# Attention with two gated MLPs on one core: two score tiles in one pair of banks, the 1e-9 added by GpSimd, the reciprocals transposed in the accumulator, and a new table of the order

## The chip, the cores and the metric

The kernel runs on one core of one Trainium2 chip. The metric is the device time of one execution in microseconds, as the median of several runs. A compute core has five engines with their own instruction streams: TensorE (PE; its weight loads are listed apart as PEld), VectorE (DVE), ScalarE (ACT), GpSimd (POOL) and SyncE (SP), which here does nothing but issue DMAs. Each engine works through its own stream in order and waits for the others by semaphores; what stands behind a waiting instruction on the same engine waits too.

## What is computed

Three stages follow each other. The first is attention with forget gates (4 batches, 8 heads, 576 positions, 64 per head), then a two-matrix MLP with softplus, then a gated MLP with a sigmoid:

```
cum    = cumsum(log(clip(f, 1e-4, 1)))
scores = q @ k.T / 8 + cum[i] - cum[j], causal
attn   = exp(scores - rowmax); attn = attn / (sum(attn) + 1e-9)
x = (attn @ v), heads side by side          # 2304 x 512
x = softplus(x @ w_in) @ w_out              # 512 -> 2048 -> 512
y = (sigmoid(x @ w_gate) * (x @ w_val)) @ w_out2
```

The weights come in as 64-bit floats and everything is computed in float32 precision: each operand is kept as a high and a low part, and a product is the sum of three matmuls.

## The kernel before

**Attention.** The 32 heads are worked through as 16 pairs, p = 0 to 15. For each pair SP loads q, k and v (`load_q`, `load_k`, `load_v`), two decay rows per head from DRAM (`decay_rows`), and POOL splits them into high and low parts (`qh`, `ql`, `kh`, `kl`, `v_high`, `v_low`). `scores` makes nine score tiles of a pair: tile i of head 0 and tile 8 - i of head 1 together for i = 0 to 3 (two PSUM banks with the tag "s", one per head, each head on 64 of the 128 rows of PE), and tile 4 for both heads in two other banks. `minimum` (DVE) adds the mask and takes the row minimum of the negated scores, `exp` (ACT) makes the exponentials and their row sums. `transposes` (PE) turns blocks of the exponentials in groups 0 to 6, `evac_h` (ACT) and `evac_l` (DVE) copy the two parts out, and `pv` (PE) multiplies by v into the accumulators `acc0` and `acc1`, which hold the transposed output of one head each.

**The reciprocals.** The output is divided by the row sums only at the end. `rinv` on DVE adds the 1e-9 (line 304, from a tile `eps` of constants) and takes the reciprocal (line 305) of 128 x 9 sums; `rinv_t` transposes them on PE into a bank of its own with the tag "t" (line 310), which it shares with the groups of `transposes`; `rinv_b` copies them to SBUF on ACT; `rinv_c` stores them to DRAM (line 319) and `rinv_d` reads them back spread over 64 partitions per head (line 325), which needs the store to have landed. `out_a` (ACT) and `out_b` (DVE) empty the accumulators, `out_c` (POOL, line 366) multiplies by the reciprocals, and `out_d` stores to the DRAM tensor xT in three DMAs (lines 373 to 375).

**Weights and tokens beside it.** While attention runs, `Weights.op` prepares the first weight blocks of the first MLP in seven steps: a load (SP, line 498), SCALE (ACT), SHIFT, LOW and SIGN (DVE, lines 520, 522, 524), HI (ACT) and LO (POOL, line 514). Ten blocks may be scaled at most before the first MLP's own loop takes over. `Tokens.step` loads the first 512 finished rows of xT (line 560) and splits them, in four chunks.

**The order.** All DMAs of attention go through SP's one queue, and all engine streams follow from the order in which the Python code emits the steps. `run` sorts the steps by a number: 9 per pair plus an entry of the table WHEN, or of START for pair 0 and END for pair 15; weights, tokens and the first two units of the first MLP have their own lists (STEPS, LATE_STEPS, X_STEPS, PRODUCTS, UNITS). Only the order of these numbers counts.

**The start.** `begin` loads the gates, makes the decay sums on DVE and ACT, and prepares pair 0's q and k. `busy` issues matmuls on a tile of zeros (line 47), 28 in all, that do no part of the computation and keep PE at work in the waits of pair 0. POOL meanwhile builds masks, the identity and other constants.

Of the kernel before, what the change touches and what calls it, by code (L numbers as in the profile page):

```python
# [9 lines left out]
F32 = mybir.dt.float32  # L10
# [3 lines left out]
ALU = mybir.AluOpType  # L14
# [7 lines left out]
class Attention:  # L22


    S = 576
# [17 lines left out]

    def busy(self, n):
# [7 lines left out]
    def begin(self):  # L52
# [12 lines left out]
        self.busy(14)  # L65
# [18 lines left out]
        nc.vector.tensor_scalar(hi, cum, -8.0, m[0:66], op0=ALU.mult, op1=ALU.mult)  # L84
        nc.vector.scalar_tensor_tensor(lo, cum, -8.0, f, op0=ALU.mult, op1=ALU.subtract)
        nc.sync.dma_start(self.nb[:, 0], c[32:64, 0:S])
        nc.sync.dma_start(self.nb[:, 1], lo[32:64].bitcast(F32))
        self.kl(P0, 0)
        self.sub(None, self.buf(P0, 0, "Xl", 640), P0["qr"], P0["Xh"], "V")
        self.constants2()  # L90

    def constants(self):
# [21 lines left out]
        self.eps = c.tile([128, 9], F32, name="eps")  # L114
        nc.gpsimd.memset(self.eps, 1e-9)
# [91 lines left out]
    def scores(self, R, p, i):  # L207
# [18 lines left out]
        w = self.W9[i]  # L226
        N = max(w, 256)
        ps = [self.ps.tile([128, 512], F32, tag="s", bufs=2, name=f"s{p}_{i}_{h}") for h in range(2)]
        q = slice(128 * i, 128 * i + 128)
        if p == 0:  # L230
            self.busy({2: 1, 3: 2}.get(i, 0))
        for j, (L, r) in enumerate(((Xh[:, q], Yh), (Xl[:, q], Yh), (Xh[:, q], Yl), (self.one[:, 0:128], nb))):
            if p == 0 and i == 1 and j == 1:
                self.busy(4)
            for h in range(2):
                o = slice(64 * h, 64 * h + 64)
                nc.tensor.matmul(ps[h][:, 0:N], L[o], r[o, 0:N], start=j == 0, stop=j == n - 1)  # L237
        for h in range(2):
            R["src", (i, 8 - i)[h]] = R["P"], ps[h][:, 0:w], self.mask[:, 512 - w:512]
# [22 lines left out]
    def transposes(self, R, p, g):  # L262
        nc = self.nc
        ps = R["T", g] = self.ps.tile([128, 512], F32, tag="t", bufs=2, name=f"t{p}_{g}")
        for n, (t, j) in enumerate(self.GROUPS[g][0]):
            if p == 0 and n == 1 and g == 3:
                self.busy(5)
            elif p == 0 and n == 0 and g == 5:
                self.busy(2)
# [98 lines left out]
    def out_d(self, R, p):  # L368
# [18 lines left out]
        ("minimum", 6): 5.8865, ("exp", 0): 6.2356, ("minimum", 2): 6.379, ("exp", 1): 6.6423, ("exp", 4): 6.7033,
        ("exp", 2): 7.105, ("transposes", 0): 7.5695, ("load_v",): 7.7728, ("exp", 6): 7.8053,
        ("transposes", 1): 7.9929, ("exp", 8): 8.7191, ("evac_h", 0): 9.5166, ("evac_h", 1): 9.5706,
        ("rinv",): 10.083, ("v_high",): 10.1126, ("evac_l", 0): 10.4436, ("v_low",): 10.514,  # L390
        ("evac_l", 1): 11.2219, ("transposes", 2): 12.2269, ("evac_h", 2): 12.276, ("transposes", 3): 12.3519,
        ("evac_h", 3): 12.4099, ("evac_l", 2): 13.0431, ("rinv_t",): 13.1193, ("rinv_b",): 13.2113,
        ("evac_l", 3): 13.7368, ("transposes", 5): 13.8096, ("transposes", 4): 13.9726, ("evac_h", 5): 14.8574,
        ("pv", 0, 0): 14.9016, ("evac_h", 4): 14.9515, ("evac_l", 5): 15.137, ("pv", 0, 2): 15.291,
        ("evac_l", 4): 15.6663, ("transposes", 6): 15.699, ("evac_h", 6): 16.5991, ("evac_l", 6): 16.839,
        ("pv", 0, 4): 17.6509, ("pv", 0, 3): 18.0197, ("pv", 0, 1): 18.5838, ("pv", 1, 0): 18.8295,
# [784 lines left out]
```

## Time and profile before

| what | value |
|---|---|
| median of 3 runs | 1022.93 us (1022.85 to 1024.15) |
| the profiled execution's own time | 1021.91 us |
| its span, first to last instruction | 1020.0 us |
| PE / PEld / DVE / ACT / POOL busy | 1006.7 / 883.1 / 610.7 / 510.4 / 147.7 us |
| DMA | 196.07 MB, 192 GB/s over the span |

Busy time of an engine is the union of its instructions; PE's matmuls overlap and their ends are modelled, so a PE that is shown as busy may still be held up inside. A row of an engine's instructions in order of time gives the start in us, the duration in us, the engine and line, the operation, out<-in with the program's names, the shape, the count, and in brackets the idle time before it and who ended it. Stretches of time are given from the start of the span. SP's rows are DMA issues.

### The profile page before, as it was taken

The numbers are of one execution on the slowest core, as the hardware profiler recorded it, in microseconds if no ns is written. First come the engines' busy times: TensorE is split into PE (matmuls) and PEld (weight loads), VectorE is DVE, ScalarE is ACT, GpSimd is POOL, SyncE is SP. The second block draws the span as 40 slices with busy tenths as digits, with TensorE's granted clock in tenths as the row PEclk, the third lists the DMA queues.
The fourth block names the chain that finished last, engine by engine and source line by source line (L and its number), as shares of the span: only waits on it lengthen the run. The fifth ranks groups of instructions, "written<-read, shape, count | busy, mean of one in ns | idle before, by whom it ended". The sixth has DMA issues, their size and how long they took to land.

```text
span 1020.0 us, 15929 instructions
## 1 busy us (share of the span) xinstructions
PE 1006.7 (99%) x5612; PEld 883.1 (87%) x5612; DVE 610.7 (60%) x1227; ACT 510.4 (50%) x1085; POOL 147.7 (14%) x154
## 2 busy tenths in 40 slices
PE   8999999999999999999999999999999999999998
PEld 6888878878788889988888889999999999999997
DVE  6999999879855766545626744544344344343333
ACT  5888888866644445435434443333333333333332
POOL 8677776610000000000000000000000000000000
PEclk9999999999999999999999999999999999999999
DMA  4455555545636566635526767766676666576641
GB/s 138 139 148 150 153 149 146 146 139 186 210 120 212 203 219 229 233 125 216 211 89 199 265 226 266 271 217 210 218 264 237 229 217 222 200 249 219 215 144 62
DMA packets 114698, 196.07 MB, mean 192 GB/s; under 512 B 14702, under 2 KB 38398, under 8 KB 114620
## 3 DMA queue, kind: packets, MB, share of 16 engines
q1 hardware_dynamic: 112684, 189.98, 55.8%
q10 hardware_dynamic: 1936, 5.09, 1.6%
q8 instruction: 44, 0.72, 0.3%
q14 instruction: 34, 0.28, 0.1%
HBM read 149.19 MB, written 45.83 MB: 191 GB/s over the span
## 4 chain that ended last, share of the span: by engine, by line
PE 86%; DVE 5%; ACT 2%; issue 2%; DMA 2%; POOL 2%; SPq 1%; ACTq 0%; POOLq 0%; DVEq 0%
PE z L577 9%; PE z L579 9%; PE z L578 9%; PE h L578 5%; PE h L577 5%; PE h L579 5%; PE x L348 4%; PE s L237 4%; PE t L272 4%; PE oY L578 2%; PE oY L577 2%; PE oY L579 2%; PE oX L578 2%; PE oX L579 2%; PE oX L577 2%
## 5 line engine op out<-in xcount | busy, mean ns | idle before, releaser
L577 PE MATMUL z<-three,three 128*128 128x384 f32 x456 | 152.9, 335 | 0.1
L579 PE MATMUL z<-three,three 128*128 128x384 f32 x456 | 152.9, 335 | 0.0
L578 PE MATMUL z<-three,three 128*128 128x384 f32 x456 | 152.7, 335 | 0.0
L626 DVE TENSOR_TENSOR gl<-L,gh 128x512 fp32r<-128x512 f32 (+1 forms) x80 | 51.0, 638 | 107.9 <-ACT gh L625 104.1
L614 ACT ACTIVATE L<-h 128x512 f32<-128x512 f32 (+1 forms) x80 | 44.3, 554 | 141.5 <-PE h L579 141.4
L577 PEld LDWEIGHTS z<-three,three 128*128 128x128 f32 x456 | 85.6, 188 | 2.0 <-DVE raw L887 0.5
L249 ACT ACTIVATE P<-P,m 128x128 f32<-128x128 f32 (+3 forms) x144 | 83.1, 581 | 7.3 <-DVE m L244 7.3
L578 PEld LDWEIGHTS z<-three,three 128*128 128x128 f32 x456 | 85.6, 188 | 1.3
L579 PEld LDWEIGHTS z<-three,three 128*128 128x128 f32 x456 | 85.6, 188 | 0.0
L244 DVE CUSTOM_DVE_ANT_0 P<-s,mask 128x256 f32<-128x256 f32 (+3 forms) x144 | 70.6, 517 | 9.9 <-PE s L237 5.9
L577 PE MATMUL h<-xh,wi_h 128*128 128x512 f32 (+1 forms) x200 | 73.7, 368 | 0.0
L579 PE MATMUL h<-xh,wi_h 128*128 128x512 f32 (+1 forms) x200 | 73.6, 368 | 0.0
L578 PE MATMUL h<-xl,wi_h 128*128 128x512 f32 (+1 forms) x200 | 73.6, 368 | 0.0
L298 DVE TENSOR_TENSOR PTl<-t,PTh 128x512 fp32r<-128x512 f32 (+2 forms) x112 | 66.8, 619 | 4.3 <-ACT PTh L294 4.2
L874 ACT COPY bl<-z 128x384 f32<-128x384 f32 x36 | 17.3, 480 | 102.4 <-PE z L579 102.4
L886 DVE TENSOR_TENSOR raw<-z,bh 128x384 f32<-128x384 f32 x36 | 20.1, 558 | 76.7 <-PE z L579 76.7
L879 DVE TENSOR_TENSOR raw<-z,p 128x384 f32<-128x384 f32 x18 | 10.0, 558 | 93.2 <-PE z L579 79.3
L294 ACT CAST PTh<-t 128x512 fp32r<-128x512 f32 (+2 forms) x112 | 55.9, 537 | 16.7 <-PE t L272 16.2
L272 PE MATMUL t<-ident,P 128*128 128x128 f32 x400 | 58.6, 280 | 3.5 <-DVE PTl L298 3.2
L908 ACT CAST gh<-raw 128x384 fp32r<-128x384 f32 x72 | 33.5, 513 | 49.0 <-DVE raw L891 47.6
L272 PEld LDWEIGHTS t<-ident,P 128*128 128x128 f32 x400 | 43.6, 140 | 16.2 <-issue 4.4
L348 PE MATMUL x<-PTh,V 128*128 128x256 f32 (+2 forms) x224 | 56.4, 312 | 0.5 <-POOL V L181 0.5
(296 smaller groups left out, 2577.1 us busy)
## 6 DMA issues: line engine op xcount, KB each, us to landing
three<-sd_g SPq DMA_DIRECT2D x126, 256.0 KB
three<-sd_v SPq DMA_DIRECT2D x126, 256.0 KB
two<-sd_w SPq DMA_DIRECT2D x36, 256.0 KB
raw_wi<-in_moe_w_in_dram SPq DMA_DIRECT2D x16, 512.0 KB
raw_wo<-in_moe_w_out_dram SPq DMA_DIRECT2D x16, 512.0 KB
fraw<-in_moe_w_gate_dram SPq DMA_DIRECT2D x12, 512.0 KB
fraw<-in_moe_w_out_dram SPq DMA_DIRECT2D x12, 512.0 KB
sd_g<-sh SPq DMA_DIRECT2D x24, 256.0 KB
```

What stands on the lines that cost most here:

```text
L237: nc.tensor.matmul(ps[h][:, 0:N], L[o], r[o, 0:N], start=j == 0, stop=j == n - 1)
L244: self.nc.vector.tensor_tensor_reduce(P, src, mask, -0.125, 3e38, op0=ALU.add, op1=ALU.min, accum_out=R["m"][:, t:t + 1])
L249: self.nc.scalar.activation(P, P, AF.Exp, bias=R["m"][:, t:t + 1], scale=-1.0, accum_out=R["sum"][:, t:t + 1])
L272: nc.tensor.transpose(ps[:, 128 * n:128 * n + 128], R["P"][:, o:o + 128], self.ident)
L294: self.nc.scalar.copy(d, s)
L298: self.nc.vector.tensor_sub(l, s, h)
L348: nc.tensor.matmul(R["acc%d" % h][:, o:o + n], v, t[:, col:col + n], start=j == 0 and w == 0, stop=j == 1 and w == 1)
L577: nc.tensor.matmul(ps, ah, bh, start=start and i == 0, stop=False, **how)
L578: nc.tensor.matmul(ps, ah, bl, start=False, stop=False, **how)
L579: nc.tensor.matmul(ps, al, bh, start=False, stop=stop and i == n - 1, **how)
L614: nc.scalar.activation(g, ph, AF.Softplus)
L626: nc.vector.tensor_sub(gl, s, gh)
```

## The change

The scores of tile 0 are written behind those of tile 1 in the same two banks (columns 256 to 511), in one call: `scores` with i = 1 now does both, and `scores` 0 is gone from the tables. The 1e-9 is added by POOL (`rinv_a`, a new step with a place of its own); DVE keeps the reciprocal. `rinv_t` writes to the first 128 columns of the pair's `acc0`, which `pv` uses from column 256 on, and not to a bank of tag "t". In `begin`, the low part of pair 0's k goes from POOL to DVE and stands with that of q ahead of the low half of the decay sums; the loads of q and k of pair 1 are issued there too. The tables are new throughout; so are the places of the idle matmuls (30). Ten weight blocks are allowed from the start, and the numbers of STEPS bring three steps of six blocks to pairs 2 to 8.

```diff
-    def rinv(self, R, p):
-        nc = self.nc
-        r = self.sm.tile([128, 9], F32, tag="r", name=f"r{p}")
-        nc.vector.tensor_add(r, R["sum"], self.eps)
-        nc.vector.reciprocal(r, r)
-        R["r"] = r
+    def rinv_a(self, R, p):
+        R["r"] = self.sm.tile([128, 9], F32, tag="r", name=f"r{p}")
+        self.nc.gpsimd.tensor_scalar(R["r"], R["sum"], 1e-9, 1.0, op0=ALU.add, op1=ALU.mult)
+
+    def rinv(self, R, p):
+        self.nc.vector.reciprocal(R["r"], R["r"])
 
     def rinv_t(self, R, p):
-        ps = self.ps.tile([128, 512], F32, tag="t", bufs=2, name=f"rt{p}")
-        self.nc.tensor.transpose(ps[0:9, 0:128], R["r"], self.ident)
-        R["rt"] = ps
+        R["acc0"] = self.wide.tile([128, 1024], F32, tag="Y", name=f"x{p}_0")
+        self.nc.tensor.transpose(R["acc0"][0:9, 0:128], R["r"], self.ident)
...
+        for x, a in ((1, 0), (0, 256)) if i == 1 else ((i, 0),):
+            w = self.W9[x]
+            N = max(w, 256)
+            q = slice(128 * x, 128 * x + 128)
+            for j, (L, r) in enumerate(((Xh[:, q], Yh), (Xl[:, q], Yh), (Xh[:, q], Yl), (self.one[:, 0:128], nb))):
...
+                    nc.tensor.matmul(ps[h][:, a:a + N], L[o], r[o, 0:N], start=j == 0, stop=j == n - 1)
...
         nc.vector.tensor_scalar(hi, cum, -8.0, m[0:66], op0=ALU.mult, op1=ALU.mult)
+        nc.sync.dma_start(self.nb[:, 0], c[32:64, 0:S])
+        P1 = self.R[1] = {}
+        self.load_q(P1, 1)
+        self.load_k(P1, 1)
+        self.sub(None, self.buf(P0, 0, "Yl", S), P0["kr"], P0["Yh"], "V")
+        self.sub(None, self.buf(P0, 0, "Xl", 640), P0["qr"], P0["Xh"], "V")
         nc.vector.scalar_tensor_tensor(lo, cum, -8.0, f, op0=ALU.mult, op1=ALU.subtract)
-        nc.sync.dma_start(self.nb[:, 0], c[32:64, 0:S])
         nc.sync.dma_start(self.nb[:, 1], lo[32:64].bitcast(F32))
-        self.kl(P0, 0)
-        self.sub(None, self.buf(P0, 0, "Xl", 640), P0["qr"], P0["Xh"], "V")
...
-    W.limit = EARLY
+    W.limit = EARLY + MORE
...
-        ("kl",): -9.0904, ("decay_rows",): -8.1126, ("scores", 4): -2.7503, ("scores", 3): -2.135,
...
-        ("rinv_c",): 19.6722, ("rinv_d",): 19.9764, ("pv", 1, 2): 20.0352, ("out_a", 0): 21.1841,
...
+        ("kl",): -0.1247, ("decay_rows",): 2.4063, ("scores", 4): 5.4379, ("scores", 3): 7.3316,
...
+        ("rinv_c",): 32.2841, ("out_b", 1): 32.2934, ("rinv_d",): 34.4816, ("out_c",): 39.1994, ("out_d",): 45.4318}
```

Below, the engines' order at three places in the middle of attention. In names like rd_1495 the number counts buffers in the built program.

SP, one period of the queue before, from one pair's store of the reciprocals (rd) to the next pair's loads (xT is the output of an earlier pair, qr, kr and vr are q, k and v, nb the decay rows):

```order
L319 DMA rd_1687<-rt_sb_1561 9x128
L325 DMA rb_1689<-rd_1687 64x576 x2
L373 DMA xT<-xs_1519 64x576
L374 DMA xT<-xs_1519 64x64
L375 DMA xT<-xs_1519 64x4x128
L148 DMA qr_124<-in_q_dram 64x576
L149 DMA qr_124<-in_q_dram 64x512
L150 DMA qr_124<-in_q_dram 64x64
L161 DMA vr_184<-in_v_dram 128x4x128
L162 DMA vr_184<-in_v_dram 64x128
L185 DMA nb_129<-nb_d 2x576 x2
L156 DMA kr_1869<-in_k_dram 64x576 x2
```

and the same period now:

```order
L316 DMA rd_1587<-rt_sb_1421 9x128
L159 DMA kr_1606<-in_k_dram 64x576 x2
L322 DMA rb_1632<-rd_1587 64x576 x2
L370 DMA xT<-xs_1345 64x576
L371 DMA xT<-xs_1345 64x64
L372 DMA xT<-xs_1345 64x4x128
L188 DMA nb_133<-nb_d 2x576 x2
L164 DMA vr_191<-in_v_dram 128x4x128
L165 DMA vr_191<-in_v_dram 64x128
L151 DMA qr_126<-in_q_dram 64x576
L152 DMA qr_126<-in_q_dram 64x512
L153 DMA qr_126<-in_q_dram 64x64
```

The load of k moved to between the store of the reciprocals and the read that needs it, and the decay rows moved to behind the stores of xT.

DVE around the reciprocals before (PTl is what `evac_l` writes, P what `minimum` writes):

```order
L244 ISA P_1023,m_1024<-s_3_1_1047,mask 128x512
L244 ISA m_1024 128x1
L304 TENSOR_TENSOR r_1103<-sum_830,eps 128x9
L305 RECIPROCAL r_1103<-r_1103 128x9
L298 TENSOR_TENSOR PTl<-t_0_1058,PTh 128x512
```

DVE now, and after it POOL around the step that makes r_939:

```order
L360 TENSOR_TENSOR xs_954<-x_0_801,bs_955 64x576
L296 TENSOR_TENSOR PTl<-t_2_934,PTh 128x512
L304 RECIPROCAL r_939<-r_939 128x9
L296 TENSOR_TENSOR PTl<-t_3_945,PTh 128x2x256
L360 TENSOR_TENSOR xs_954<-x_1_903,bs_955 64x576
```

```order
L184 TENSOR_TENSOR Yl_879<-kr_833,Yh_877 128x576
L184 TENSOR_TENSOR V_842<-vr_189,V_842 128x10x64
L301 TENSOR_SCALAR r_939<-sum_626 128x9
L363 TENSOR_TENSOR xs_761<-xs_761,rb_859 128x576
```

The addition left DVE, and the reciprocal now stands behind a step of POOL that itself follows the low parts of k and v.

PE at score tile 0 before, after a block of `pv` on all 128 rows and ahead of the transpose of the reciprocals:

```order
L348 MATMUL x_1_1092<-PTl,V_911 128x256
L237 MATMUL s_0_0_1163<-Yh_878,Xh_849 128x256
L237 MATMUL s_0_1_1164<-Yh_878,Xh_849 128x256
L237 MATMUL s_0_0_1163<-Yh_878,Xl_882 128x256
L237 MATMUL s_0_1_1164<-Yh_878,Xl_882 128x256
L237 MATMUL s_0_0_1163<-Yl_885,Xh_849 128x256
L237 MATMUL s_0_1_1164<-Yl_885,Xh_849 128x256
L237 MATMUL s_0_0_1163<-nb_130,one 128x256
L237 MATMUL s_0_1_1164<-nb_130,one 128x256
L310 MATMUL rt_1174<-ident,r_1103 9x128
L272 MATMUL t_5_1182<-ident,P_828 128x128 x4
```

and now, from the end of tile 1 to the end of the first two terms of tile 0:

```order
L239 MATMUL s_1_0_1110<-nb_133,one 128x256
L239 MATMUL s_1_1_1111<-nb_133,one 128x256
L239 MATMUL s_1_0_1110<-Yh_877,Xh_871 128x256
L239 MATMUL s_1_1_1111<-Yh_877,Xh_871 128x256
L239 MATMUL s_1_0_1110<-Yh_877,Xl_873 128x256
L239 MATMUL s_1_1_1111<-Yh_877,Xl_873 128x256
```

Tile 0's eight matmuls moved to directly behind tile 1's, so PE goes from 128 rows to 64 and back three times per pair, and not four.

## Rows read from the trace of the kernel before

**Rows 1.** Busy time by stretch: length, PE, PEld, DVE, ACT, POOL (instructions), PE clock, DMA share, GB/s.
```profile
28.69:122.24 93.55, 93.35 (x750) 78.29 (x749) 89.53 (x240) 83.72 (x233) 66.48 (x59) 1.00 0.52 143
122.24:184.68 62.44, 59.39 (x475) 49.39 (x473) 59.40 (x158) 53.17 (x146) 45.72 (x39) 1.00 0.52 148
184.68:296.92 112.24, 110.14 (x559) 91.31 (x558) 92.18 (x173) 73.06 (x140) 14.70 (x12) 1.00 0.50 167
296.92:1020.00 723.08, 719.24 (x3696) 646.54 (x3694) 350.24 (x611) 285.32 (x532) 0.00 (x0) 1.00 0.60 208
```
**Rows 2.** PE in order of time: first matmul of score tile 4, pairs 2, 3, 15.
```profile
28.69 0.40 PE L222 MATMUL s<-Yh,Xh 128*128 128x288 f32 x1
...
40.22 0.29 PE L222 MATMUL s<-Yh,Xh 128*128 128x288 f32 x1
...
184.68 0.29 PE L222 MATMUL s<-Yh,Xh 128*128 128x288 f32 x1
```
**Rows 3.** SP in order of time, 100.57 to 111.90: one period of the queue.
```profile
100.57 0.44 SPq L319 DMA_DIRECT2D rd<-rt_sb  x1
103.67 1.09 SPq L325 DMA_DIRECT2D rb<-rd  x2
...
110.69 1.11 SPq L156 DMA_DIRECT2D kr<-in_k_dram  x2
111.90 0.44 SPq L319 DMA_DIRECT2D rd<-rt_sb  x1
...
120.50 0.59 SPq L498 DMA_DIRECT2D raw_wi<-in_moe_w_in_dram  x1
121.14 0.43 SPq L161 DMA_DIRECT2D vr<-in_v_dram  x1
```
**Rows 4.** Waits of the SP queue, 0 to 220: us in total, times, longest.
```profile
SPq L325 <- DMA rd<-rt_sb: 30.2, 13, 4.2
```
**Rows 5.** DVE groups by shape, 28.69 to 122.24: count | busy us, mean ns | idle before.
```profile
L304 DVE TENSOR_TENSOR r<-sum,eps 128x9 f32<-128x9 f32 x8 | 8.1, 1014 | 0.0
L305 DVE RECIPROCAL r<-r 128x9 f32<-128x9 f32 x8 | 1.7, 216 | 0.3
L522 DVE SCALAR_TENSOR_TENSOR w_wo<-raw_wo,w_wo 128x512 uint32<-128x512 uint32 x1 | 0.8, 819 | 0.0
```
**Rows 6.** DVE and POOL in order of time, around one addition.
```profile
56.16 0.96 DVE L304 TENSOR_TENSOR r<-sum,eps 128x9 f32<-128x9 f32 x1
...
55.66 1.43 POOL L366 TENSOR_TENSOR xs<-xs,rb 128x576 f32<-128x576 f32 x1
```
**Rows 7.** PE in order of time, the block of a 256-column score tile.
```profile
33.59 0.39 PE L237 MATMUL s<-Yh,Xh 64*128 64x256 f32 x2
33.81 0.28 PE L237 MATMUL s<-Yh,Xl 64*128 64x256 f32 x2
33.93 0.28 PE L237 MATMUL s<-Yl,Xh 64*128 64x256 f32 x2
...
34.26 0.30 PE L348 MATMUL x<-PTh,V 128*128 128x64 f32 x1
```
**Rows 8.** The start, in order of time: DVE, POOL, PE.
```profile
6.66 1.93 DVE L85 SCALAR_TENSOR_TENSOR nb<-decays 66x576 fp32r<-66x576 f32 x1
8.51 0.81 DVE L181 TENSOR_TENSOR Xl<-qr,Xh 128x640 fp32r<-128x640 f32 x1
...
6.56 1.41 POOL L181 TENSOR_TENSOR Yl<-kr,Yh 128x576 fp32r<-128x576 f32 x1 [1.84 <-ACT Yh L175]
...
12.44 0.65 PE L237 MATMUL s<-Yh,Xh 64*128 64x384 f32 x2
```
**Rows 9.** The chain of waits, 8 to 11: start us, us, what.
```profile
8.57 1.27 POOL mask L122
...
9.89 0.67 POOL mask L122
```
**Rows 10.** PE in order of time, pair 15's tail: the transpose of its reciprocals.
```profile
205.72 0.28 PE L310 MATMUL rt<-ident,r 128*9 128x128 f32 x1 [1.52 <-DVE PTl L298]
```

More of the change, by code (lines that the diff above doesn't have):

```diff
@@ L41, in pools @@
         self.io = io_pool("at_io", 2)
+    BUSY = {("scores", 3): 4, ("transposes", 1): 6}
     def busy(self, n):
@@ L64, in begin @@
         self.spare = self.wide.tile([128, 1024], F32, tag="Y", name="spare")
-        self.busy(14)
+        self.busy(17)
         nc.sync.dma_start(c[0:32, 0:S], row(0, 32))
@@ L225, in scores @@
             return
-        w = self.W9[i]
-        N = max(w, 256)
         ps = [self.ps.tile([128, 512], F32, tag="s", bufs=2, name=f"s{p}_{i}_{h}") for h in range(2)]
[L229 to L234, printed above, removed]
+        for x, a in ((1, 0), (0, 256)) if i == 1 else ((i, 0),):
[3 more added lines that the diff above has]
+            for j, (L, r) in enumerate(((Xh[:, q], Yh), (Xl[:, q], Yh), (Xh[:, q], Yl), (self.one[:, 0:128], nb))):
+                if p == 0 and (x, j) == (1, 1):
+                    self.busy(3)
+                for h in range(2):
+                    o = slice(64 * h, 64 * h + 64)
+                    nc.tensor.matmul(ps[h][:, a:a + N], L[o], r[o, 0:N], start=j == 0, stop=j == n - 1)
             for h in range(2):
[L236 to L239, printed above, removed]
+                R["src", (x, 8 - x)[h]] = R["P"], ps[h][:, a:a + w], self.mask[:, 512 - w:512]
     def minimum(self, R, p, t):
@@ L265, in transposes @@
         for n, (t, j) in enumerate(self.GROUPS[g][0]):
[L266 to L269, printed above, removed]
             o = self.O9[t] + 128 * j
@@ L387 @@
[L387 to L396, printed above, removed]
@@ new lines @@
+        ("scores", 2): 12.9741, ("exp", 1): 14.3071, ("minimum", 2): 15.3051, ("exp", 7): 15.4776,
+        ("minimum", 6): 15.8604, ("exp", 0): 16.1403, ("v_high",): 16.3129, ("exp", 2): 16.3206, ("exp", 6): 16.8725,
+        ("transposes", 0): 17.5068, ("exp", 8): 17.7926, ("transposes", 1): 18.0407, ("evac_h", 0): 18.2375,
+        ("evac_h", 1): 18.5430, ("evac_l", 0): 19.4950, ("evac_l", 1): 19.6439, ("v_low",): 19.8168,
+        ("transposes", 2): 19.9725, ("rinv_a",): 20.0073, ("transposes", 3): 20.3092, ("evac_h", 2): 21.1753,
@@ L443, in run @@
         ops = [(self.PERIOD * p + edge.get(p, {}).get(op, r), i, p, op) for p in range(self.NP)
-               for i, (op, r) in enumerate(self.WHEN.items()) if p or op[0] not in self.FIRST]
+               for i, (op, r) in enumerate(self.WHEN.items()) if op[0] not in self.FIRST[:(7, 2)[p] if p < 2 else 0]]
         ops += [(t, -1, i, f) for i, (t, f) in enumerate(others)]
@@ L449, in run @@
             else:
+                if p == 0:
+                    self.busy(self.BUSY.get(op, 0))
                 getattr(self, op[0])(self.R.setdefault(p, {}), p, *op[1:])
@@ L1035 @@
         others += [(end + t, lambda k=k: x1.step(0, k)) for k, t in enumerate(X_STEPS)]
-        others += [(end - .5, open_pools), (end + 18.1, W.alone)]
+        others += [(end + 6.6099, open_pools), (end + 500, W.alone)]
         others += [(end + t, lambda u=u: m1[1].product(u)) for u, t in enumerate(PRODUCTS)]
-        others += [(end + 8.3, lambda: nc.scalar.preload_act_table_set("softplus"))]
+        others += [(end + 27.0954, lambda: nc.scalar.preload_act_table_set("softplus"))]
         others += [(end + t, lambda u=u: m1[1].unit(u, 0)) for u, t in enumerate(UNITS)]
```

100 lines of the change are left out of this document (53 added, 47 removed), and 18 rows, old and new, of tables (END, STEPS, WHEN).

## The prediction
> **What bounds the kernel now.** I began with the busy time by stretch [rows 1] and cut the span where score tile 4 of a pair begins on PE, since that block comes once a pair [rows 2]. The reader should see four parts. Up to 28.69 us lies the start. From 28.69 to 122.24 lie eight pairs in 93.55 us, 11.69 each, with three engines nearly full: PE 93.35, DVE 89.53, ACT 83.72. From 122.24 to 184.68 lie five pairs in 62.44 us, 12.49 each, with PE busy only 59.39 and DVE 59.40, although a pair's attention is the same work as before. Then come 112.24 us of pair 15, and 723.08 us of MLP with PE busy 719.24. The shortest pair takes 40.22 - 28.69 = 11.53 us [rows 2].
>
> What lengthens the second group shows on no compute engine, so I read SP next. In one period of its queue the store of the reciprocals is issued at 100.57, the read-back only at 103.67, the next store at 111.90 [rows 3]: 11.33 us, of which 3.10 pass from store to read. The list of waits names the store's landing there: 30.2 us in 13 waits [rows 4], 2.3 a pair, in which nothing else can be issued. Each load added to the queue takes another 0.64 (120.50 to 121.14 [rows 3]). By SP's order the eight pairs have three weight loads more, so the queue alone needs 11.33 + 3 x 0.64/8 = 11.57 a pair, and the five pairs have four weight loads and two token loads more, 11.33 + 6 x 0.64/5 = 12.10, plus waits of token loads for xT. That is close to the 11.69 and the 12.49 measured. **The queue sets the pace of the five pairs and stands level with PE in the eight.**
>
> **The change, part by part.** The sum is made against the profiled execution, 1021.91 us; the median, 1022.93, lies 1.02 above it, and the differences are applied to the median. About 0.2%, 2.0 us, is what a measurement can tell.
>
> *The load of k* moves into the wait between store and read. It occupies 111.90 - 110.69 = 1.21 us of the queue [rows 3], so the period falls to 10.12. Six weight loads come in the eight pairs now: 10.12 + 6 x 0.64/8 = 10.6. Two weight loads and four token loads come in the five: 10.9. Both are under what PE needs, so SP stops being the bound. What is late next: the decay rows, now behind the read-back and the stores of xT. From the store to their issue I count 3.10 + 1.09 + 3 x 0.64 + 2 x 0.64 = 7.4 us, and with a landing as long as the store's (3.10; 4.2 the longest [rows 4]) 10.5 to 11.6 us. The table puts them at 2.41 for a score tile 4 at 5.44, and the store of three pairs earlier at 32.28, which is 5.28: tile 4 of the next pair stands about one period, 11.4, behind a store. The slack is 0.9 us, or nothing in the longest case.
>
> *The addition* leaves DVE: eight of them took 8.1 us, mean 1014 ns, and the reciprocal of the same shape 216 ns [rows 5]. The addition is short work that is held: 56.16 + 0.96 ends where POOL's multiplication by the reciprocals does, 55.66 + 1.43 = 57.09 [rows 6]. The reciprocal never shows this. DVE gains 1.0 us a pair. On POOL I take 0.2, the reciprocal's price; bounds nothing and the 1.0 that DVE paid. It stands behind the low part of v, which `pv` needs in any case; waiting for it are the reciprocal on DVE, and behind that evacuations and minima.
>
> *The weights* take most of that back in the eight pairs: SHIFT, LOW and SIGN of six blocks instead of about seven such steps. One takes 0.82 [rows 5]. DVE then has (89.53 - 8.1 - 5.7)/8 = 9.46 plus 18 x 0.82/8 = 1.85: 11.3 a pair, and 11.8 with the idle time that it has now, (93.55 - 89.53)/8 = 0.5. In the five pairs it is relieved. Two more blocks get these three steps ahead of the MLP, 4.9 us of DVE work that PE hides there; I take nothing, and at best 1.0 of the 3.84 that PE idles in that stretch [rows 1].
>
> *Tiles 0 and 1 in one bank.* A block of tile 0 takes 34.26 - 33.59 = 0.67 on PE, while its later passes follow at 33.93 - 33.81 = 0.12 [rows 7]: four make 0.48, and 0.2 goes to the change between 64 and 128 rows. One such change goes per pair. The minima of tile 1 now also wait for tile 0's 0.48; two banks make their round well inside a period, so it costs nothing unless DVE is full there. The idle matmuls stand in pair 0's waits: nothing.
>
> PE's period is thus 11.53 - 0.2 = 11.33, or 11.13 if the change is paid going and coming. For the **eight pairs** I take 11.45, between PE's 11.33 and DVE's 11.3 to 11.8, nearer the shortest pair seen: 93.55 - 91.6 = **-1.95** (bounds 8 x 11.13: -4.5, and 8 x 11.8: +0.9). For the **five pairs** I take PE's 11.3: 62.44 - 56.5 = **-5.9** (bounds 11.13: -6.8, and the 59.39 that PE is busy now: -3.0).
>
> *The start.* The low half of the decay sums takes DVE from 6.66 to 8.59, held by POOL's low part of k (6.56 + 1.41 = 7.97), and Xl ends at 9.32 [rows 8]. Now DVE makes both low parts first: 0.8 + 0.81 + the 0.62 that the held step needs after 7.97, from 6.63: 8.9, some 0.4 sooner. One round of the banks ahead of tile 2 (12.44 [rows 8]) falls away with tile 0's own block, about 1. I take **-1.5**; the low end is the whole 1.3 of the hold and two blocks of 0.67: -2.7. Against it: POOL's masks, until now behind its low part of k, start earlier and run beside DVE's three steps. One mask step took 1.27 beside Xl and 0.67 alone [rows 9]; if DVE waits for two of them, 2 x 0.67, and the bank's round brings nothing, the start is 1.34 - 0.4 = 0.9 longer: the upper end, +0.9.
>
> A rule speaks against this part. The Trainium skill, "SBUF — State Buffer", section "SBUF: two separate sides", says that a DVE operation with two SBUF inputs and a GpSimd operation share a pair of ports under an exclusive lock, and that the loser waits for the whole instruction. The trace agrees: the addition (two SBUF inputs) ended with POOL's multiplication [rows 6] and the reciprocal was free; and the low parts, with two inputs each, would be held by the masks, which would make the start that of the second rival below rather than -1.5.
>
> *The tail.* PE idles 112.24 - 110.14 = 2.1 us in pair 15 [rows 1], 1.52 of it ahead of the transpose of the reciprocals, which waits for a bank that DVE's PTl frees [rows 10]. That wait cannot recur in the accumulator. The tail's table is new throughout and may open another: **-1.0**, bounds -2.1 and +2.1.
>
> Sum: -1.95 - 5.9 - 1.5 - 1.0 = -10.35. Profiled 1011.5, **median 1012.5**.
>
> **The rivals.**
> *The weights crowd DVE and ACT in the eight pairs*, which stay at 11.7; start and tail cancel. For it: DVE at 96% before, and the 11.8 above. Against: the queue is freed there too. Only the five pairs gain: 1022.93 - 5.9 = 1017.0.
> *The start is held by POOL's masks*: +0.9 in place of -1.5: 1014.9. For it: the 1.27 against 0.67. Against: the masks may be over when DVE gets there.
> *The change does not do what it says*: the queue's wait was hidden, and the five pairs are long because token loads wait for xT itself. Then only tile 0's 13 x 0.2 = 2.6 goes, against a tail that may lose as much: 1023, give or take 2. Against it: PE idles 3 us in the five pairs and its work is no more than in the eight.
> *Slower: the decay rows come late in every pair.* Their slack is 0.9, and nothing with the 4.2 landing. PE then stands at tile 4, whose last pass needs them, and all behind it. If all 13 pairs ran as the five with late loads do, 13 x 12.49 = 162.4 against 155.99 now: +6.4; with the start's and tail's -2.5, 1026.8. It decides from 10.35/13 = 0.8 us of lateness a pair.
>
> **How the numbers follow.** Forecast 0.48; weights crowding 0.17; start held 0.15; no effect 0.08; slower 0.12. The forecast's low ends together are -4.5 - 6.8 - 2.7 - 2.1 - 1.0 = -17.1, so the range begins at 1006. Upward it takes in both milder rivals, the first with the five pairs at their upper end: 1022.93 - 3.0 = 1020. Outside lie the last two, 0.2. Faster 0.48 + 0.17 + 0.15 = 0.80, same 0.08, slower 0.12.
>
> **What would show it.** Score tile 4 should recur every 11.3 to 11.5 us in both groups. SP's waits for the store should fall from 2.3 to about 1.1 each. There should be no addition on DVE, a POOL addition near 0.2, and the reciprocal still at 216 ns. Tile 2 should start before 12.44 and pair 2's tile 4 some 1.5 before 28.69; the 1.52 in the tail should be gone. I am wrong on the queue if the five pairs stay above 12 us while SP waits less; wrong on the rest if PE is seen waiting for the decay rows at tile 4, or for POOL's addition ahead of the transpose of the reciprocals.

## The result and the profile after

The changed kernel takes 1012.67 us (median of 4 runs, 1012.59 to 1012.84), the kernel before, with a fourth run, 1023.54. The ratio is 0.9894, with a 95% interval of 0.9877 to 0.9911: about 1.1% faster. The predicted time was 1012.5. **The number held, and the largest of its reasons did not**; the runs below show which.

The stretches of the kernel after, cut at the same places as [rows 1] (length, PE, PEld, DVE, ACT, POOL with instructions, PE clock, DMA share, GB/s):

```profile
0.00:25.96 25.96, 23.53 (x146) 17.77 (x146) 18.13 (x49) 15.93 (x40) 20.79 (x47) 1.00 0.67 186
25.96:118.92 92.96, 89.72 (x747) 78.07 (x747) 89.55 (x239) 86.35 (x233) 78.00 (x71) 1.00 0.57 158
118.92:177.54 58.62, 56.62 (x473) 49.30 (x472) 53.96 (x147) 52.53 (x144) 43.35 (x41) 1.00 0.56 155
177.54:287.87 110.33, 109.08 (x560) 91.85 (x559) 89.41 (x167) 70.86 (x139) 14.69 (x13) 1.00 0.47 153
287.87:1010.95 723.08, 719.19 (x3697) 646.70 (x3695) 350.11 (x611) 285.40 (x532) 0.00 (x0) 1.00 0.61 208
```

| stretch | before | after | difference | forecast |
|---|---|---|---|---|
| start, to score tile 4 of pair 2 | 28.69 | 25.96 | -2.73 | -1.5 |
| eight pairs | 93.55 | 92.96 | -0.59 | -1.95 |
| five pairs | 62.44 | 58.62 | -3.82 | -5.9 |
| pair 15 and the beginning of the first MLP | 112.24 | 110.33 | -1.91 | -1.0 |
| the rest | 723.08 | 723.08 | 0 | 0 |

The four differences make -9.05, where -10.35 were forecast. The medians differ by 10.9 because the profiled execution of before (1021.91) lay 1.6 below the median of its four runs, while that of after (1012.74) lay at its median; the forecast time was hit with the help of that.

**A plain pair shows the gain best.** It is one that no step of weights or tokens lengthens. In before, 11.64 us is the usual period of the eight pairs, and (run 5) that of a pair without such steps. First matmul of score tile 4, two pairs in succession, before:

```profile
98.79 0.29 PE L222 MATMUL s<-Yh,Xh 128*128 128x288 f32 x1
...
110.43 0.29 PE L222 MATMUL s<-Yh,Xh 128*128 128x288 f32 x1
```

and two pairs, and then two others, after:

```profile
59.52 0.38 PE L225 MATMUL s<-Yh,Xh 128*128 128x288 f32 x1
...
72.86 0.38 PE L225 MATMUL s<-Yh,Xh 128*128 128x288 f32 x1
...
107.79 0.38 PE L225 MATMUL s<-Yh,Xh 128*128 128x288 f32 x1
...
118.92 0.38 PE L225 MATMUL s<-Yh,Xh 128*128 128x288 f32 x1
```

A plain pair fell from 11.64 to 11.13: 13 x 0.51 = 6.6 us. But the pair from 59.52 takes 13.34. Above 13 plain pairs, before spent 93.55 + 62.44 - 13 x 11.64 = 4.7 us and after 92.96 + 58.62 - 13 x 11.13 = 6.9. So 2.2 us of the gain were given back. DVE's groups in the eight pairs after (count | busy us, mean ns | idle before) say to whom:

```profile
L524 DVE SCALAR_TENSOR_TENSOR w_wi<-raw_wi,w_wi 128x512 uint32<-128x512 uint32 x3 | 4.3, 1428 | 0.0
L522 DVE SCALAR_TENSOR_TENSOR w_wo<-raw_wo,w_wo 128x512 uint32<-128x512 uint32 x3 | 3.0, 1008 | 0.0
L304 DVE RECIPROCAL r<-r 128x9 f32<-128x9 f32 x8 | 1.6, 199 | 0.0
```

The reciprocal is what it was (199 ns; 216 in [rows 5]) and the addition is gone from DVE; on POOL it takes 289 ns. But a step of the weights, 0.82 in [rows 5], now takes up to 2.0 us. Here are such steps on DVE, the first elsewhere and the second in the pair of 13.34, and then what POOL and PE did beside the second:

```profile
50.14 0.69 DVE L522 SCALAR_TENSOR_TENSOR w_wi<-raw_wi,w_wi 128x512 uint32<-128x512 uint32 x1
...
61.58 1.59 DVE L524 SCALAR_TENSOR_TENSOR w_wi<-raw_wi,w_wi 128x512 uint32<-128x512 uint32 x1
...
61.20 1.43 POOL L184 TENSOR_TENSOR Yl<-kr,Yh 128x576 fp32r<-128x576 f32 x1
...
63.79 1.06 PE L270 MATMUL t<-ident,P 128*128 128x128 f32 x8 [0.88 <-DVE PTl L296]
```

The step at 61.58 ends at 63.17, and POOL's low part of k at 62.63: as I read it, the step stood until POOL was done, and then took its own 0.5. Behind it DVE came late with `PTl`, and PE stood 0.88 us for that. It is the hold of [rows 6], now on the weights. The pairs from 59.52 and from 72.86 (12.37) have two steps of 1.49 to 1.66 us each; together they hold 3.45 of the 3.92 us by which the eight pairs exceed eight plain ones.

The queue did what was forecast and more. SP's wait for the store, of 30.2 us in [rows 4], after:

```profile
SPq L322 <- DMA rd<-rt_sb: 8.9, 8, 2.6
```

### The profile page after: what moved, and what is told of

The parts are those of the page before. It is cut to its first block, busy times and chain, and to the rows that moved or that the text cites. A ratio compares the mean times of both kernels' runs of the same rounds, so it can differ in the third digit from the quotient of the medians.

```text
span 1010.9 us, 15938 instructions
## 1 busy us (share of the span) xinstructions
PE 998.1 (99%) x5614; PEld 883.7 (87%) x5614; DVE 601.2 (59%) x1210; ACT 511.1 (51%) x1085; POOL 156.8 (16%) x170
## 4 chain that ended last, share of the span: by engine, by line
PE 91%; DVE 5%; DMA 2%; SPq 1%; issue 1%; ACT 0%; DVEq 0%
PE z L577 9%; PE z L579 9%; PE z L578 9%; PE h L578 6%; PE h L577 6%; PE h L579 6%; PE x L345 4%; PE t L270 3%; PE s L239 3%; PE oY L578 3%; PE oY L579 3%; PE oY L577 3%; PE o L578 2%; PE o L577 2%; PE o L579 2%; PE oX L577 2%
## 5 line engine op out<-in xcount | busy, mean ns | idle before, releaser
L251 ACT ACTIVATE P<-P,m 128x576 f32<-128x576 f32 (+3 forms) x144 | 83.5, 581 | 5.5 <-DVE m L246 4.9
L246 DVE CUSTOM_DVE_ANT_0 P<-s,mask 128x256 f32<-128x256 f32 (+3 forms) x144 | 68.5, 513 | 9.4 <-PE s L239 8.6
L270 PE MATMUL t<-ident,P 128*128 128x128 f32 x400 | 63.1, 281 | 5.5 <-DVE PTl L296 5.4
L345 PE MATMUL x<-PTh,V 128*128 128x320 f32 (+2 forms) x224 | 57.5, 311 | 0.3 <-ACT rt_sb L312 0.3
L345 PE MATMUL x<-PTl,V 128*128 128x320 f32 (+2 forms) x224 | 54.2, 292 | 0.0
L727 DVE TENSOR_TENSOR l<-fw,sh 128x512 fp32r<-128x512 f32 x60 | 40.7, 686 | 14.2 <-ACT sh L726 7.2
L625 ACT CAST gh<-L 128x512 fp32r<-128x512 f32 (+1 forms) x80 | 46.2, 578 | 2.5
```

Source lines behind the costliest of these rows:

```text
L246: self.nc.vector.tensor_tensor_reduce(P, src, mask, -0.125, 3e38, op0=ALU.add, op1=ALU.min, accum_out=R["m"][:, t:t + 1])
L251: self.nc.scalar.activation(P, P, AF.Exp, bias=R["m"][:, t:t + 1], scale=-1.0, accum_out=R["sum"][:, t:t + 1])
L345: nc.tensor.matmul(R["acc%d" % h][:, o:o + n], v, t[:, col:col + n], start=j == 0 and w == 0, stop=j == 1 and w == 1)
L625: nc.scalar.copy(gh, s)
```

## The experiments

Each was measured against runs of the kernel before on the same chip. That kernel's medians lay between 1022.2 and 1023.7 there, so ratios and stretches are compared rather than times.

**1 and 2. The load of k alone.** One number in the table of before, and one in that of after:

```diff
-        ("load_k",): -16.9757
+        ("load_k",): -16.2
```
```diff
-        ("load_k",): -2.4877
+        ("load_k",): -3.75
```

> The kernel before, with one number changed: the load of k stands behind the store of the reciprocals instead of ahead of it. Theory (the queue's empty wait of 2.3 us a pair lengthens the five late pairs): the wait for the store shrinks to about 1.1 us, the five pairs fall from 62.4 to 57 to 59 us, the eight pairs by at most 1 us, the time to 1018 to 1020. Rival (the wait was hidden, DVE's held addition sets the five pairs): five pairs 62 to 63 us, time within 2 us of the kernel before.

> The changed kernel with the load of k put back ahead of the store of the reciprocals. Theory: the wait for the store comes back (over 2 us a pair), the queue's period rises by 1.2 us, the five pairs go from 58.6 back to 60 to 62 us, the eight from 93.0 to 93 to 95, the time to 1014 to 1018. Rival: no stretch changes by over 1 us and the time stays at 1012 to 1013.5.

Measured: 0.9997 (0.9989 to 1.0006) for before with the load in the gap. Waits of the SP queue and the two groups of pairs:

```profile
SPq L325 <- DMA rd<-rt_sb: 15.1, 9, 3.6
```
```profile
28.89:122.46 93.57, 93.37 (x749) 78.34 (x748) 89.59 (x240) 83.74 (x233) 66.58 (x59) 1.00 0.50 143
122.46:186.05 63.59, 59.61 (x475) 49.45 (x473) 60.76 (x158) 53.62 (x148) 47.70 (x40) 1.00 0.52 151
```

The queue's wait was halved, from 30.2 to 15.1, and no pair gained. The five pairs even grew by 1.15, all of it in the last of them (13.08 and not 11.93), where a SIGN step on DVE took 1.96 us and not 0.69. In the other direction, after with the load ahead of the store: 0.9908 (0.9895 to 0.9921), waits 21.3 and not 8.9, and the pairs at 92.93 and 58.64 against 92.96 and 58.62:

```profile
SPq L322 <- DMA rd<-rt_sb: 21.3, 14, 2.7
```
```profile
25.85:118.78 92.93, 89.69 (x748) 78.05 (x747) 89.49 (x240) 86.37 (x233) 77.97 (x71) 1.00 0.56 160
118.78:177.42 58.64, 56.61 (x473) 49.29 (x472) 53.97 (x147) 52.52 (x144) 43.36 (x41) 1.00 0.54 155
```

**The queue's wait was hidden in both kernels.** My theory falls; the rival of the first run is right as far as it speaks of the wait (its five pairs, 62 to 63, came to 63.59, and its held addition is not tested here).

**3 and 4. The addition alone.** Before with the addition on POOL, behind the low part of v, and after with the addition on DVE:

```diff
...
-        nc.vector.tensor_add(r, R["sum"], self.eps)
-        nc.vector.reciprocal(r, r)
...
+        nc.vector.reciprocal(R["r"], R["r"])
...
+    def rinv_a(self, R, p):
+        R["r"] = self.sm.tile([128, 9], F32, tag="r", name=f"r{p}")
+        self.nc.gpsimd.tensor_scalar(R["r"], R["sum"], 1e-9, 1.0, op0=ALU.add, op1=ALU.mult)
...
-        ("rinv",): 10.083, ("v_high",): 10.1126, ("evac_l", 0): 10.4436, ("v_low",): 10.514,
+        ("v_high",): 10.1126, ("evac_l", 0): 10.4436, ("v_low",): 10.514, ("rinv_a",): 10.515, ("rinv",): 11.2220,
```
```diff
...
-        self.nc.gpsimd.tensor_scalar(R["r"], R["sum"], 1e-9, 1.0, op0=ALU.add, op1=ALU.mult)
...
+        self.nc.vector.tensor_add(R["r"], R["sum"], self.eps)
         self.nc.vector.reciprocal(R["r"], R["r"])
```

> The kernel before, with the 1e-9 added by GpSimd behind the low part of v and the reciprocal one place later on DVE; order, queue and banks otherwise as before. Theory: DVE loses 8 x 1.0 us of work in the eight pairs, of which PE sees at most 2 us; the five pairs stay at 62 to 63 us because the queue sets them; time 1021 to 1023. Rival (DVE's addition sets the five pairs): five pairs below 59 us and a time below 1019.

> The changed kernel with the addition of 1e-9 back on DVE, with two inputs in SBUF, directly ahead of the reciprocal. Theory (DVE is held until GpSimd's multiplication ends, and DVE is full in the eight pairs): one such row near 1 us a pair, the eight pairs 1 to 5 us longer than 93.0, the five pairs at most 2 us longer than 58.6, time 1014 to 1018. Rival (the addition is hidden on DVE): time within 1 us of 1012.7.

Before with the addition on POOL is slower: 1.0175 (1.0162 to 1.0189), eight pairs 101.49, five 72.03. DVE's waits, from 25 to 235 us:

```profile
DVE r L303 <- POOL r L307: 31.6, 14, 6.5
```

In that order POOL makes the low part of v too late, and DVE stands for the addition behind it. Neither theory had this, and the run doesn't tell what the addition on DVE cost in before.

After with the addition on DVE takes 0.9986 (0.9978 to 0.9994) of before; nearly all of the gain is gone, more than I had allowed (1018, and 5 us in the eight pairs). Its two groups of pairs, and DVE's groups in the first:

```profile
26.97:126.39 99.42, 92.85 (x747) 79.63 (x746) 96.47 (x247) 87.44 (x233) 75.49 (x63) 1.00 0.52 147
126.39:185.71 59.32, 57.93 (x473) 50.16 (x472) 54.80 (x152) 52.89 (x144) 42.12 (x36) 1.00 0.53 153
```
```profile
L527 DVE SCALAR_TENSOR_TENSOR w_wi<-raw_wi,w_wi 128x512 uint32<-128x512 uint32 x3 | 5.4, 1797 | 0.0
L525 DVE SCALAR_TENSOR_TENSOR w_wo<-raw_wo,w_wo 128x512 uint32<-128x512 uint32 x3 | 4.7, 1576 | 0.0
L306 DVE TENSOR_TENSOR r<-sum,eps 128x9 f32<-128x9 f32 x8 | 2.7, 335 | 0.0
```

The addition takes only 335 ns here and not the 1 us expected, 2.7 us in eight pairs. But DVE now meets POOL at other times: the same two groups of weight steps grow from 1428 and 1008 to 1797 and 1576 ns, and all 16 weight steps of the eight pairs from 16.1 to 20.8 us. The eight pairs lose 6.5 us and the five 0.7: DVE is nearly full where the weights are (96.47 of 99.42), and has room where they are not (54.80 of 59.32).

**5 and 6. No weight steps on DVE.** In both kernels SHIFT, LOW and SIGN of the first eight blocks are left out:

```diff
-            self.bits(s, u, lo, hi)
+            if self.at[s] > 8:
+                self.bits(s, u, lo, hi)
```

> The kernel before without the DVE steps SHIFT, LOW and SIGN of the first eight weight blocks; the loads, SCALE, HI and LO stay. It leaves out the assembly of those weights. New theory (the queue did not set the late pairs; DVE's SBUF-only steps, held up by GpSimd's two-input steps, did): the five late pairs fall from 62.4 to 58.5 to 60 us, that is 11.7 to 12 each, though SP issues what it did before; the eight pairs stay at 92.5 to 93.6; time 1017 to 1020. Rival (PE waits in the late pairs for something else, such as loads and GpSimd): five pairs still over 61 us.

> The changed kernel without the DVE steps SHIFT, LOW and SIGN of the first eight weight blocks; the rest stays. It leaves out the assembly of those weights. New theory: every pair without such a step took 11.13 us, so the eight pairs come to 89 to 89.7 us instead of 92.96 and the five to 55.7 to 57.2 instead of 58.62; time 1006 to 1009. Rival (the two periods of 13.3 and 12.4 us have another cause): the eight pairs stay over 92.

Before, 0.9968 (0.9956 to 0.9979), and after, 0.9841 (0.9827 to 0.9854):

```profile
28.56:122.09 93.53, 93.33 (x750) 78.13 (x748) 84.95 (x232) 83.84 (x233) 66.48 (x59) 1.00 0.51 141
122.09:182.01 59.92, 58.80 (x474) 49.44 (x473) 53.37 (x150) 52.81 (x146) 43.80 (x39) 1.00 0.52 152
```
```profile
25.84:114.24 88.40, 88.40 (x747) 77.50 (x747) 76.14 (x223) 85.20 (x233) 73.69 (x71) 1.00 0.61 169
114.24:170.14 55.90, 55.90 (x474) 48.88 (x472) 49.50 (x144) 52.42 (x144) 42.86 (x41) 1.00 0.57 158
```

This is what sets the long pairs. In before the eight pairs do not move; the longest weight step there took 0.82. The five fall by 2.5 of the 4.2 us that they stand above plain pairs, while SP's wait for the store stays (30.5 us, with 30.2 in [rows 4]). Of the 2.5, 1.13 and 1.16 come from the two pairs that had a step of 1.75 or 1.76 us. This is the first of them in before, with POOL beside it:

```profile
123.29 1.75 DVE L522 SCALAR_TENSOR_TENSOR w_wo<-raw_wo,w_wo 128x512 uint32<-128x512 uint32 x1
...
122.91 1.57 POOL L181 TENSOR_TENSOR Xl<-qr,Xh 128x640 fp32r<-128x640 f32 x1
```

The steps went whole, so these runs do not part the hold from the step's own 0.69. In after the eight fall by 4.6 and the five by 2.7, a little more than expected (88.40 where 89 was the low end), and PE has no gap left. Of the 1.7 us that remain in before's five, 1.4 sit in the two pairs with a conversion of tokens; that was not taken apart.

**7. Tile 0 in a turn of its own**, right behind the minima of tile 1 (they and tile 0 stand at 11.27 to 11.61 in the table):

```diff
-        for x, a in ((1, 0), (0, 256)) if i == 1 else ((i, 0),):
+        for x, a in ((i, 0),):
...
+        ("exp", 5): 11.5456, ("minimum", 1): 11.6046, ("scores", 0): 11.6050, ("minimum", 8): 11.6638, ("minimum", 0): 11.8131,
```

The tables of pairs 0 and 15 get tile 0 in the same way, and there the minimum of tile 7 moves ahead too.

> The changed kernel with score tile 0 in a turn of the banks of its own again, right behind the minima of tile 1 in the order. Theory (one change between 128 and 64 rows of PE is saved by the merge): a plain pair 0.1 to 0.4 us longer than 11.13, time 1014 to 1019. Rival (the merge is free of effect on the pair): plain pairs at 11.1 to 11.2, time 1012.5 to 1013.5. A turn of the banks that PE must wait for would show as more than 0.5 a pair.

1.0035 (1.0023 to 1.0048): some 13 us above the changed kernel, far over the 1019 expected. Plain pairs take 11.64 again, 0.51 more where 0.1 to 0.4 was expected. That is just over the 0.5 that was to betray a wait for the banks, but in the pair read here (91.85 to 103.49) no wait of PE shows. PE's rows show where the time goes. Tile 0 apart, and then tile 1 with tile 0 behind it in the changed kernel:

```profile
98.71 0.66 PE L270 MATMUL t<-ident,P 128*128 128x128 f32 x4
99.29 0.39 PE L239 MATMUL s<-Yh,Xh 64*128 64x256 f32 x2
99.51 0.28 PE L239 MATMUL s<-Yh,Xl 64*128 64x256 f32 x2
...
99.75 0.28 PE L239 MATMUL s<-nb,one 64*128 64x256 f32 x2
99.96 0.38 PE L345 MATMUL x<-PTh,V 128*128 128x256 f32 x1
```
```profile
113.75 0.29 PE L239 MATMUL s<-nb,one 64*128 64x256 f32 x2
113.86 0.29 PE L239 MATMUL s<-Yh,Xh 64*128 64x256 f32 x2
...
114.21 0.29 PE L239 MATMUL s<-nb,one 64*128 64x256 f32 x2
114.43 0.66 PE L270 MATMUL t<-ident,P 128*128 128x128 f32 x4
...
115.07 0.65 PE L270 MATMUL t<-ident,P 128*128 128x128 f32 x4
115.48 0.36 PE L345 MATMUL x<-PTh,V 128*128 128x256 f32 x1
```

From four transposes to what follows, 98.71 to 99.29 is 0.58 if 64 rows follow and 115.07 to 115.48 is 0.41 if not: 0.17. The first pass of tile 0 takes 0.22 and behind tile 1 0.12: 0.10. Its last takes 0.21, 0.09 more than a pass between others. That is 0.36 for one excursion to 64 rows and back, entry and exit. Of the remaining 0.15, the ends of the blocks of tiles 3 and 2 took 0.11 and 0.07 longer than in the changed kernel, and the rest of the pair a little less; why is not shown. The 13 pairs lose 6.6 us by the 0.51. The other 6 us of this run are not the merge in a plain pair: the pairs with weight steps grew by more (up to 14.16), the start by 1.7, and pair 15 with the MLPs by 1.6.

**8, 9 and 10. The weight steps elsewhere.** First behind the minima, where POOL idles (2.86 in a pair's nine units); then ahead of the minima of tiles 0 and 1, where DVE waits for scores and POOL's multiplication is about over (1.70); then there with three token conversions too:

```diff
-         (56.8230, 2), (61.2523, 4), (61.9264, 5), (64.2165, 3), (64.3033, 6), (64.3246, 0), (65.4674, 1),
...
+         (61.9300, 5), (64.3000, 6), (64.3246, 0), (65.4674, 1), (65.8600, 2), (65.8700, 3), (74.8600, 4), (74.8700, 2),
```
```diff
+         (61.9300, 5), (64.3000, 6), (64.3246, 0), (64.7000, 2), (64.7100, 3), (65.4674, 1), (73.7000, 4), (73.7100, 2),
```
```diff
-X_STEPS = [-55.9659, -35.7404, -22.6778, -20.8793, -16.8314, -15.9540, -9.6352, -2.5455]
+X_STEPS = [-55.9659, -34.2900, -22.6778, -16.2900, -16.2800, -7.2900, -7.2800, 1.7100]
```

> The changed kernel with all of its work, the DVE steps of the weights moved to the place in a pair where GpSimd idles, behind the last minimum of tiles 0 and 1 and ahead of the first emptying of an accumulator, two per pair in pairs 2 to 13; two conversions of tokens moved there too. New theory: the steps take 0.4 to 0.8 us and not 1.5, the eight pairs fall to 89 to 91 us, the five to 56 to 57.5, time 1008 to 1010.5. Rival (DVE has no room for two steps in one place, whatever their length): eight pairs 92 to 94, time 1012 to 1014.

> The changed kernel with all of its work, the DVE steps of the weights moved to another place in a pair: behind the low part of group 1 and ahead of the minima of tiles 0 and 1, where DVE waits 1.1 us or more for PE's scores and GpSimd's multiplication by the reciprocals is over; one or two per pair in pairs 2 to 13. New theory (a step costs PE what it adds to DVE at a place where DVE is late, and its length depends on GpSimd): steps of 0.4 to 0.7 us, eight pairs 89 to 91 us, five pairs 56 to 58.5 (the tokens' conversions stay where they are held), time 1007 to 1010. Rival (any two steps in a pair cost a pair its full length, as behind the minima): eight pairs 92 to 96, time 1012 to 1017.

> The same, with three of the four conversions of tokens on DVE moved to that place too. New theory: the held conversion of 1.5 us goes, the five pairs come to 56 to 57 us, time another 0.5 to 1.5 us lower, 1006 to 1009. Rival: no difference beyond 0.5 us, because the conversions wait for something else.

The first: 0.9948 (0.9934 to 0.9961), slower than the changed kernel, although nearly all steps were short, 10.2 us in the eight pairs and not 16.1:

```profile
L522 DVE SCALAR_TENSOR_TENSOR w_wo<-raw_wo,w_wo 128x512 uint32<-128x512 uint32 x3 | 2.1, 692 | 0.1
```
```profile
25.85:121.52 95.67, 89.13 (x748) 78.27 (x747) 84.79 (x239) 85.39 (x232) 74.61 (x71) 1.00 0.57 158
```

The rival holds here, and its numbers (92 to 94, 1012 to 1014) are even passed: at a place from which the evacuations and the reciprocal follow, two steps of 1.1 to 1.9 us in all cost a pair 0.4 to 1.1. The second: 0.988 (0.9864 to 0.9897), eight pairs 91.24 (just over the 89 to 91 expected), five 56.80, attention 3.5 us shorter to pair 15. Each of the eight pairs has two steps, and five of them took 11.13 to 11.17, some with a step held, as the first below, although 0.4 to 0.7 had been expected of a step:

```profile
54.30 1.26 DVE L524 SCALAR_TENSOR_TENSOR w_wo<-raw_wo,w_wo 128x512 uint32<-128x512 uint32 x1
...
66.51 1.79 DVE L524 SCALAR_TENSOR_TENSOR w_wi<-raw_wi,w_wi 128x512 uint32<-128x512 uint32 x1
...
65.99 1.76 POOL L363 TENSOR_TENSOR xs<-xs,rb 128x576 f32<-128x576 f32 x1
```

(The pair of the last two rows took 12.40: a low part of weights had come first on POOL, and the multiplication ran only at 65.99.) So the place counts before the length. The changed kernel has such a case itself: a SIGN of 2.01 us at 26.89, in a pair of 11.31. The time, 1011.54, is over the 1007 to 1010 expected and not clear of the changed kernel's: the intervals overlap. Behind attention, from the last product with v to the second MLP, the changed kernel took 386.30 us with PE never idle and this one 390.27:

```profile
202.40:592.67 390.27, 388.07 (x1888) 327.68 (x1886) 243.14 (x427) 187.23 (x334) 2.96 (x2) 1.00 0.55 194
```

The profiled execution, 1013.36, was the slowest of its four, so at its median up to 1.8 us less may be given back.

The third, 0.9913 (0.9898 to 0.9928), is slower than the second, against theory and rival: 1014.53, eight pairs 91.25, five 57.54. The five pairs account for 0.7 of the 3 us; where the rest went is not shown.

**11. The start**, with the low part of pair 0's k on POOL again:

```diff
-        self.sub(None, self.buf(P0, 0, "Yl", S), P0["kr"], P0["Yh"], "V")
...
+        self.kl(P0, 0)
```

> The changed kernel with the low part of pair 0's k back on GpSimd, ahead of its masks, and the low half of the decay sums ahead of the low part of q on DVE, as in the kernel before. Theory of the prediction: the held step takes about 1.9 us again, score tile 4 of pair 2 moves from 25.96 to between 26.4 and 28 us, time 0.5 to 2 us up. Rival (the start gained by the order of the tiles and the earlier loads of pair 1 alone): tile 4 of pair 2 stays at 25.7 to 26.3 us.

0.9904 (0.9889 to 0.9918), and score tile 4 of pair 2 at 26.13 and not 25.96, although the low half of the decay sums took 1.99 us once more: 0.17 us, the rival. In the changed kernel DVE's three steps there end at 9.41, and before at 9.32: nothing was gained on DVE. POOL's first step for pair 1, before and after, shows what came earlier instead:

```profile
14.33 0.72 POOL L173 TENSOR_SCALAR Xh<-qr 128x640 fp32r<-128x640 f32 x1 [0.50 <-DMA qr<-in_q_dram]
```
```profile
11.10 0.73 POOL L176 TENSOR_SCALAR Xh<-qr 128x640 fp32r<-128x640 f32 x1 [0.86 <-DMA qr<-in_q_dram]
```

Pair 1's q, loaded from `begin`, came 3.2 us earlier, and pair 1's tile 4 moved from 20.55 to 17.38. That the loads did this is read from the trace; they were not moved back alone. Run 7 kept them early, and its start took 27.62 all the same, 1.66 of the 2.73 lost again. So tile 0's place in pairs 0 and 1 (moved there together with the minimum of tile 7) has its share too, and no run parts the two.

**12. Two loads of weights earlier**, as number 9, with the steps of blocks 6 and 7 in pairs 10 to 14 and the loads numbered among them:

```diff
+         (118.7000, 3), (118.7100, 4), (119.0000, 0), (127.7000, 2), (127.7100, 3), (128.0000, 0), (136.7000, 4), (138.0000, 0)]
```

> As the run with the weights' DVE steps ahead of the minima, and besides: no step in pair 2; the steps of blocks 6 and 7 done in pairs 10 to 14 too, so that two more loads of weights go out during attention. In the run before, attention ended 3.5 us earlier than in the changed kernel, and the first MLP gave 4.0 back: PE stood there for weights that were still being loaded. Theory (the MLP waits for loads that wait for their buffers): attention ends 3 to 4 us earlier than in the changed kernel, at most 1 us of waits on PE remains in the first MLP, time 1007 to 1009.5. Rival (the loads' own transfer time sets the first MLP's pace, whenever they are issued): 1011 to 1013.

0.9957 (0.9943 to 0.9971), eight pairs 98.50, five 59.27: worse than theory and rival, and for a reason of its own. I had delayed the steps of the first blocks by a pair, so the fifth load had to wait for its buffer, in SP's queue, with v behind it. SP's waits from 40 to 105 us, and POOL:

```profile
SPq L498 <- DVE w_wi L524: 15.3, 2, 9.8
...
60.21 0.72 POOL L176 TENSOR_SCALAR V<-vr 128x640 fp32r<-128x640 f32 x1 [6.55 <-DMA vr<-in_v_dram]
```

The pair from 58.84 took 15.56 us. Here I take the queue to have set the pace: 9.8 us are too many where the 3.1 of [rows 3] cost nothing. The part behind attention took 386.30 again, with no wait on PE; that fits the theory on the loads, but behind an attention that ended 5.9 us later than in the changed kernel it does not prove it.

## Why the prediction was right and wrong

**The queue.** "The queue sets the pace of the five pairs and stands level with PE in the eight" is the step that failed. The sum of issues and landing, 12.10 and 11.57, came near the periods measured, and I took nearness for cause. Runs 1 and 2 halve the wait or more than double it, and no stretch follows it. A queue that always has its next issue ready a pair ahead also shows a period equal to the kernel's, whatever sets it. The reading ahead of it, "shows on no compute engine", failed too: of the 3.0 us that PE idles in before's five pairs, 2.5 end with DVE's `PTl` (six waits), and DVE has weight steps of 1.75 and 1.76 us there (run 5). The -5.9 was -3.82, from the shorter plain pair (5 x 0.51 = 2.6) and from less waiting above it.

**The merge of tiles 0 and 1** was mis-sized: 0.2 a pair, with 0.4 "if the change is paid going and coming" as the low end, PE at 11.13. It is paid both ways: 0.36 by rows, 0.51 in the plain pair, 11.13 exactly. By this term alone 6.6 us were gained where I put 2.6.

**The weights** were spread too evenly. 18 x 0.82 makes 14.8 us of DVE work in the eight pairs; the 16 steps that fell there took 16.1, so the total was off by little. But the average over eight pairs hid that four of the longest steps stand together in two of them, and the hold that I had just read from the addition was not counted at all. Plain pairs at 11.13 would have given 8 x 0.56 = 4.5; 3.9 went back, and 0.59 was left where I put 1.95. The rival of weights crowding DVE was half right: the eight pairs hardly moved, but start and tail did not cancel.

**The rule on the shared ports** (the Trainium skill, "SBUF — State Buffer", section "SBUF: two separate sides") was weighed at the start, where run 11 gives it 0.17 us, and not at the weights, where steps of 0.69 took up to 2.0. This page of the Trainium skill counts as locked out not only DVE operations with two SBUF inputs but also those in a two-port mode. The trace agrees in so far as SHIFT, with one input, took 1.02 and 0.41 in the pair of 13.34, and the evacuations of 128x512, with an input in PSUM, never over 0.69; whether SHIFT runs in such a mode no run shows.

**The addition** on POOL takes 0.2 to 0.5 there, and no wait of PE for it shows in the pairs, as forecast. Its worth is not the 1.0 a pair that DVE showed: without it on DVE, run 7's plain pair takes the same 11.64 as before's, and in the new order its 0.3 costs 9 us (run 4). **The decay rows** came in time: no PE wait for them shows in the pairs. **The start** was right in sign; of its reasons, the held step is worth 0.17 (run 11), tile 0's own turn fits run 7 (1.66 where about 1 was put), and the earlier loads of pair 1 had not been counted. **The tail's** pause is gone from the transpose of the reciprocals, and pair 15 waits 0.72 and 0.34 us elsewhere: PE's idle time fell from 2.10 to 1.25. The rest of the -1.91 is 1.06 us less of PE work, which the term did not have; part of it will be pair 15's own merge.

So the time was hit by luck: errors of +2.1, +1.4, -1.2 and -0.9 us left only +1.3, and the step of 1.02 between a profiled execution and a median, which the kernel after did not have, made up for most of that.

## What to carry to other kernels

A wait in a queue is worth what moves when it is taken away: halve it alone before believing in it, however well its period fits. Look for DVE steps that work only in SBUF and stretch when GpSimd does the same; try a place for them where DVE is waiting anyway. Here short steps where others follow cost more than held ones where nobody does (runs 8 and 9), though what run 9 gained in attention did not show clearly in the time. And an edit and the order around it are one change: the same addition cost 9 us or 18 us in the wrong order.

## What was not expected of the hardware

A wait on PE can be paid twice. In run 12, PE stood for 1.62 us up to 98.62 and was busy for 0.70 of the 2 us from 96.00, and in the next stretch the granted clock was 0.60 in the mean, so that most of it ran at the lower level of 1.2 GHz:

```profile
96.00:98.00 2.00, 0.70 (x5) 0.42 (x4) 0.30 (x1) 1.29 (x5) 1.95 (x2) 1.00 0.47 139
98.00:100.68 2.68, 2.06 (x11) 2.06 (x11) 2.35 (x6) 0.18 (x2) 2.57 (x4) 0.60 0.66 192
```

In run 3 the two longest pairs (14.71 and 18.16 us) had 0.88 and 0.81. The pair from 59.52 in the changed kernel, with waits below 1 us, kept 1.00. So part of what these two runs lost is clock, and their differences overstate the waits.
